# A state-space layer and a gated MLP: the last group's last product laid out by tokens, and the accumulators' copies written ahead of each group's last product

## The chip, the core and the metric

One core of a Trainium2 chip runs the whole program: TensorE (PE), which multiplies and writes its sums to PSUM; VectorE (DVE), ScalarE (ACT) and GpSimd (POOL), which compute on SBUF and PSUM; SyncE (SP), which here only issues transfers; and 16 DMA engines. The metric is the time of one execution on the device in microseconds, the median over several executions. The trace comes from one profiled execution. In it a 32-bit matmul shows as two passes, each with its weight load (PEld).

## The reference

A chunked state-space scan (4 batches, 8 heads, 768 steps, head size 32, state size 16) makes `y`; its heads, put side by side, are the 3072 tokens of 256 features that go into a two-layer network of 2048 hidden units with the activation `h * sigmoid(1.702 h)`.

```python
def reference(x, a, B, C, moe_w_in, moe_w_out):
    y = ssd(x, a, B, C)              # (4, 8, 768, 32), in chunks of 32 steps
    x = y.transpose(0, 2, 1, 3).reshape(3072, 256)
    h = x @ moe_w_in                 # (256, 2048)
    g = h * (1.0 / (1.0 + np.exp(-1.702 * h)))
    return g @ moe_w_out             # (2048, 256) -> (3072, 256)
```

All is in float32; the two weight matrices come as float64 and are made float32 on the chip.

## The kernel before

The tokens run in six groups of 512 (`TG`, `NG` = 6). For each group the scan makes `yT` (features on partitions, tokens along the row), the first layer makes the hidden blocks `gT[g, j]` (`j` from 0 to 7, 256 hidden units each), and the second layer adds eight products into accumulators in PSUM.

From group 2 on in the first layer, and from group 1 on in the second, a 2x2 block product is made with seven multiplications in place of eight. `mix_w` and `mix_g` make sums of blocks of `w_out` and of `gT` beforehand (`mw`, `mg`). `product(g, j, only)` (L809) issues the chosen ones of seven terms, each a matmul of 128x128 weights with 128 rows of 256 tokens, into seven accumulators of 128x256. For groups 1 to 4 the seven lie in one PSUM tile of four banks (`acc{g}`, from `area`, one buffer, the same that the scan's scores `cb` use). For group 5 they lie in four tiles of two. `ORDER` (L807) is 0, 1, 5, 4, 2, 3, 6. The accumulators have output features on partitions and tokens along the row.

After a group's last product, `combine(g)` (L849) makes the four output blocks. It first calls `copies(g)` (L834), in which ScalarE copies accumulators 0 and 3 from PSUM to SBUF (L840, one activation of 128x512). Then VectorE makes five sums (`plus`, L847) into `u` and `c`. `give(g)` turns the blocks of `c` back to tokens on partitions with TensorE transposes (`turn_out`, L864), scales them on ScalarE (L872) and stores them.

The order of work is written out by hand: the strings given to `run` name each step. `P` is the next product of the group before, `j.i` is term `i` of the first layer's block `j` of this group, and letters stand for other calls. `in_order` makes every engine issue its instructions in program order. In the string of L1121 the last product (`P`, term 6 of `j` = 7) stands ahead of `1.D C`: `1.D` is a VectorE sum into `gT[g, 1]`, and `C` calls `combine(g - 1)`. `block(g, 1)` takes the `gT` buffer at `1.D`; `copies` takes two more of the same six. After that come first-layer steps (`2.1 1.S 1.4 1.3 2.6 ...`, L733 and L743), and `s1`, the next scores (L546), which need the PSUM tile of the accumulators.

The last group is finished by `end` (L876). It makes the last three `j` (5, 6, 7) of all seven terms, term by term, so that the sums of one term run while TensorE makes the next. Its order of terms is 0, 3, 4, 2, 6, 1 and 5. Term 5 is made in two halves of 128 tokens (`products(5, halves[k])`), each followed by a VectorE sum of that half. Then all blocks of `c` are turned (`o[0]`: both feature blocks of the first 256 tokens; `o[2]` and `o[1]`: the two feature blocks of the last 256 tokens), scaled, and stored by three transfers: `store` from SP (L761), `put` from ScalarE's queue and `put` from SP's (L883).

Of the kernel before, what the change touches and what calls it, by code (L numbers as in the profile page):

```python
# [35 lines left out]
def kernel(  # L36
# [31 lines left out]
    nc = tc.nc  # L68
# [12 lines left out]
    NF = DF // P  # L81
    NG = T // TG
# [12 lines left out]
    ffn = ctx.enter_context(tc.tile_pool(name="ffn", bufs=2))  # L95
# [164 lines left out]
    for r in range(R):  # L260
# [22 lines left out]
                            op1=ALU.min)  # L283
# [203 lines left out]
    def bank(name):  # L487
        return ps.tile([P, 4 * P], FP32, tag="ff", name=name)
# [316 lines left out]


    ORDER = (0, 1, 5, 4, 2, 3, 6)  # L807

    def product(g, j, only=ORDER, cols=slice(0, HT)):  # L809
        if j == 0 and g not in acc:  # L810
            if g < NG - 1:
                a = area(f"acc{g}").rearrange("p r (t e) -> p (r t) e", t=2)
                acc[g] = [a[:, i] for i in range(7)], a
            else:

                areas.close()
                last = ctx.enter_context(
                    tc.tile_pool(name="last", bufs=1, space=bass.MemoryType.PSUM))
                tiles = [last.tile([P, 2, HT], FP32, name=f"acc{g}_{i}") for i in range(4)]
                acc[g] = [tiles[i // 2][:, i % 2] for i in range(7)], tiles  # L820
        B = gT[g, j].rearrange("p i (t e) -> p i t e", t=2)
        T = mixed_g[g, j]
        A, S = w_out[:, 2 * j:2 * j + 2], mixed_w[j]

        terms = ((A[:, 0, :P], B[:, 0, 0]), (A[:, 1, :P], B[:, 1, 0]), (S[:, 1], T[:, 2]),
                 (S[:, 0], T[:, 0]), (S[:, 2], T[:, 1]), (S[:, 3], B[:, 1, 1]),
                 (A[:, 1, P:], T[:, 3]))
        for i in only:
            lhsT, rhs = terms[i]
            nc.tensor.matmul(out=acc[g][0][i][:, cols], lhsT=lhsT, rhs=rhs[:, cols],  # L830
                             start=(j == 0 and i in (0, 2, 5, 6)), stop=(j == NF // 2 - 1),
                             skip_group_check=True)

    def copies(g):  # L834
        u = ffn.tile([P, 4, HT], FP32, tag="gT", name=f"u{g}", bufs=6)
        c = ffn.tile([P, 2, 2, HT], FP32, tag="gT", name=f"c{g}", bufs=6)
        done[g] = u, c

        if g < NG - 1:
            nc.scalar.activation(u[:, 0:4:3], acc[g][1][:, 0:4:3], AF.Copy)  # L840
        else:
            nc.scalar.activation(u[:, 0], acc[g][0][0], AF.Copy)
            nc.scalar.activation(u[:, 3], acc[g][0][3], AF.Copy)
        return u, c

    def plus(o, v, w):
        nc.vector.tensor_tensor(out=o, in0=v, in1=w, op=ALU.add)  # L847

    def combine(g):  # L849


        u, c = copies(g)
        a = acc[g][1]
        plus(u[:, 2], a[:, 2], u[:, 0])
        plus(u[:, 1:3], a[:, 3:5], u[:, 2:3].to_broadcast([P, 2, HT]))
        plus(c[:, 1, 1], u[:, 2], u[:, 3])
        plus(c[:, 0], a[:, 1:6:4], u[:, 0:2])
        plus(c[:, 1, 0], a[:, 6], u[:, 2])

    def turn_out(g, t, blocks, o, ks=range(2)):  # L860

        for i in blocks:
            for k in ks:
                nc.tensor.transpose(out=o[:, k, i * P:(i + 1) * P],  # L864
                                    in_=done[g][1][:, i, t, k * P:(k + 1) * P], identity=ident)

# [8 lines left out]

    def end(g, j0):  # L876

        def products(i, cols=slice(0, HT)):
            for j in range(j0, NF // 2):
                product(g, j, (i,), cols)  # L880

        def put(k0, k1, i, ob, queue):
            queue.dma_start(  # L883
                out=out[g * TG + HT + k0 * P:g * TG + HT + k1 * P, i * P:(i + 1) * P].rearrange(
                    "(k p) d -> p k d", p=P), in_=ob[:, k0:k1])

        _, p2, p6, p5, p7, p3, p4 = acc[g][0][:7]
        products(0)
        products(3)
        u, c = copies(g)  # L890
        u2, u4, u3 = u[:, 2], u[:, 1], c[:, 1, 0]
        products(4)
        products(2)
        plus(u2, p6, u[:, 0])
        plus(u4, p5, u2)
        products(6)
        plus(u3, p7, u2)
        plus(c[:, 1, 1], u3, u[:, 3])
        products(1)
        plus(c[:, 0, 0], p2, u[:, 0])  # L900
        o = [bank(f"oT{g}_{i}").rearrange("p (k e) -> p k e", k=2) for i in range(3)]
        ob = [ffn.tile([P, 2, TG], FP32, tag="gT", name=f"ob{g}_1_{i}", bufs=6)[:, :, :P]
              for i in range(2)]
        halves = [slice(k * P, (k + 1) * P) for k in range(2)]
        products(5, halves[0])
        plus(c[:, 1, 0], p4, u3)
        plus(c[:, 0, 1, halves[0]], p3[:, halves[0]], u4[:, halves[0]])
        products(5, halves[1])
        plus(c[:, 0, 1, halves[1]], p3[:, halves[1]], u4[:, halves[1]])
        turn_out(g, 0, range(2), o[0])  # L910
        half_out = out_tile(g, 0)
        nc.scalar.activation(half_out, o[0], AF.Copy, scale=1.0 / GELU_SCALE)
        store(g, 0, half_out)
        turn_out(g, 1, (1,), o[2])
        nc.scalar.activation(ob[1], o[2][:, :, P:], AF.Copy, scale=1.0 / GELU_SCALE)
        put(0, 2, 1, ob[1], nc.scalar)
        turn_out(g, 1, (0,), o[1])
        nc.vector.tensor_single_scalar(out=ob[0], in_=o[1][:, :, :P], scalar=1.0 / GELU_SCALE,
                                       op=ALU.mult)
        put(0, 2, 0, ob[0], nc.sync)  # L920


    assert PG == 2
# [166 lines left out]
    def seven(g, j):  # L1090
        return [(g, j, (i,)) for i in ORDER]

# [16 lines left out]
    for g in range(2, NG):  # L1109
        n, p = (g + 1) * PG, (g + 2) * PG  # L1110
        more, most = g + 1 < NG, g + 2 < NG
        chunks = list(range((g + 2) * CG, (g + 3) * CG)) if most else []
        rows = [b for b in range(NB) if most and (g + 2) * CG <= b * NC < (g + 3) * CG]
        if most:
            load(p)
            for c in chunks[:2]:
                spread(c)
            for b in rows:
                spread_rows(b)
        run(g, "0.1 P P 0.6 P P 0.7 P 0.5 P 0.2 P 0.D", seven(g - 1, 6))  # L1120
        run(g, "1.1 0.S P 0.4 P P 1.6 P 0.3 0.T P 1.5 P 1.7 1.2 P 1.D C", seven(g - 1, 7),  # L1121
            C=lambda: combine(g - 1))
        def along():
            for r in rows:
                clip_rows(r)
                decay_rows(r)

        def refill():
            if most:
                load(p + 1)  # L1130
                for c in chunks[2:]:
                    spread(c)

        if more:

            run(g, "2.1 1.S 1.4 1.3 2.6 2.5 2.2 2.7 1.T s1 2.D 2.S w1 give 2.4 3.1 2.3 3.5 2.T M0 3.6 "
                "s2 w2 y1 refill 3.7 3.2 3.D along 4.1 P P 3.4 P 3.S 4.6 P 3.3 4.5 3.T M1 P P y2 4.7 P 4.2 4.D M2",
                seven(g, 0), s1=lambda: score(n), w1=lambda: weigh(n), give=lambda: give(g - 1),
                s2=lambda: score(n + 1), w2=lambda: weigh(n + 1), y1=lambda: finish(n),
                refill=refill, along=along, y2=lambda: finish(n + 1), M0=lambda: mix_g(g, 0), M1=lambda: mix_g(g, 1),  # L1140
                M2=lambda: mix_g(g, 2))
            if most:
                decay(chunks[0])
        else:
# [51 lines left out]
```

## Time and profile before

| | |
|---|---|
| median of 4 runs | 374.63 us (374.59 to 374.76) |
| profiled execution: time, span of the trace | 374.6 us, 372.9 us |
| granted TensorE clock | 1.000 |
| `copies` in `combine` (L840), 4 times | 597 ns each; ScalarE idle before them 2.0 us in all, until TensorE L830 |
| VectorE's first sum (L847) after it, 4 times | idle before 1.3 us in all, until L840 |
| scores (L546) that wait for `combine`'s sums, 3 times | TensorE idle 1.1 us in all |
| products L830, `acc<-mg,mw`, 128x256 | 240 passes, mean 379 ns |
| products L830 of 128x128 in `end` | 12 passes, from 365.66 and from 366.87 us |
| the last three stores, issued | 368.95, 369.23 and 369.42 us |

How to read it: a row of the timeline has start, duration, engine, line, operation, `output<-inputs`, and in brackets how long the engine was idle before it and what ended that. Consecutive instructions of one kind are merged (`x2`), from the first start to the last end. A matmul's duration holds its way through the array, so consecutive ones overlap: 256 columns take 0.38 us each, and start 0.216 us after one another. The list of waits has the time waited in all, how often, and the longest.

### The profile page before, as it was taken

The numbers are of one execution on the slowest core, as the hardware profiler recorded it, in microseconds if no ns is written. First come the engines' busy times: TensorE is split into PE (matmuls) and PEld (weight loads), VectorE is DVE, ScalarE is ACT, GpSimd is POOL, SyncE is SP. The second block draws the span as 40 slices with busy tenths as digits, with TensorE's granted clock in tenths as the row PEclk, the third lists the DMA queues.
The fourth block names the chain that finished last, engine by engine and source line by source line (L and its number), as shares of the span: only waits on it lengthen the run. The fifth ranks groups of instructions, "written<-read, shape, count | busy, mean of one in ns | idle before, by whom it ended". The sixth has DMA issues, their size and how long they took to land.

```text
span 372.9 us, 5764 instructions
## 1 busy us (share of the span) xinstructions
PE 364.2 (98%) x2278; PEld 285.1 (76%) x2278; DVE 267.7 (72%) x439; ACT 152.0 (41%) x337; POOL 10.8 (3%) x34
## 2 busy tenths in 40 slices
PE   7999999999999999999999999999999999999995
PEld 3674468885467588778888788888878888888884
DVE  4999999998879976587886476888484355464443
ACT  5678661402331123553433554423554331554320
POOL 4200000100000010000000000000000000000000
PEclk9999999999999999999999999999999999999999
DMA  9997698806856110086300073000010000000011
GB/s 153 243 347 131 229 228 121 247 9 112 186 140 115 58 42 0 2 169 114 112 3 1 2 132 94 0 2 0 0 58 2 0 3 1 0 2 0 0 58 56
DMA packets 85795, 29.56 MB, mean 79 GB/s; under 512 B 75721, under 2 KB 79241, under 8 KB 85769
## 3 DMA queue, kind: packets, MB, share of 16 engines
q1 hardware_dynamic: 83320, 28.81, 32.8%
q10 hardware_dynamic: 2448, 0.39, 0.6%
q8 instruction: 18, 0.29, 0.3%
q14 instruction: 9, 0.07, 0.1%
HBM read 25.95 MB, written 3.24 MB: 78 GB/s over the span
## 4 chain that ended last, share of the span: by engine, by line
PE 91%; DVE 5%; ACT 2%; DMA 1%; issue 1%; ACTq 0%; DVEq 0%
PE acc L830 33%; PE X L733 13%; PE h L661 13%; PE Y L743 10%; PE o L773 8%; PE cb L546 3%; PE y L619 3%; DVE c L847 2%; PE y L610 2%; PE h L675 1%; PE ab L462 1%; PE tp L498 1%; DVE u L847 1%; PE oT L864 1%; ACT L L481 1%; PE A L574 1%
## 5 line engine op out<-in xcount | busy, mean ns | idle before, releaser
L830 PE MATMUL acc<-mg,mw 128*128 128x256 f32 x240 | 66.0, 379 | 0.0
L847 DVE TENSOR_TENSOR gT<-Y,ac 128x512 f32<-128x512 f32 x32 | 22.1, 691 | 44.3 <-PE Y L743 42.4
L738 ACT ACTIVATE ac<-X 128x256 f32<-128x256 f32 x64 | 24.6, 384 | 66.5 <-PE X L733 66.4
L830 PEld LDWEIGHTS acc<-mg,mw 128*128 128x128 f32 x240 | 45.6, 190 | 6.2
L661 PE MATMUL h<-yT,w_in 128*128 128x512 f32 x112 | 49.9, 595 | 0.0
L710 ACT ACTIVATE gT<-gT 128x512 f32<-128x512 f32 x64 | 33.3, 521 | 28.2 <-DVE gT L847 27.8
L830 PE MATMUL acc<-gT,w_out 128*128 128x256 f32 x160 | 43.8, 380 | 0.0
L347 DVE TENSOR_TENSOR_SCAN L<-a,idents 128x1024 f32<-128x1024 f32 x18 | 41.1, 2283 | 0.0
L733 PE MATMUL X<-my,mi 128*128 128x256 f32 x128 | 38.7, 384 | 0.0
L661 PEld LDWEIGHTS h<-yT,w_in 128*128 128x128 f32 x112 | 20.8, 190 | 23.4 <-issue 21.4
L830 PEld LDWEIGHTS acc<-gT,w_out 128*128 128x128 f32 x160 | 30.2, 190 | 5.5 <-issue 1.4
L847 DVE TENSOR_TENSOR gT<-Y,b 128x256 f32<-128x256 f32 x32 | 13.5, 422 | 26.7 <-PE Y L743 26.4
L664 ACT ACTIVATE gT<-h 128x512 f32<-128x512 f32 x28 | 16.6, 596 | 39.4 <-PE h L661 39.3
L773 PE MATMUL o<-w_out,gT 128*128 128x256 f32 x128 | 29.0, 382 | 0.0
L701 DVE TENSOR_TENSOR mg<-gT 128x512 f32<-128x512 f32 x40 | 27.3, 682 | 0.0
L733 PEld LDWEIGHTS X<-my,mi 128*128 128x128 f32 x128 | 23.7, 190 | 4.3 <-issue 1.2
L773 PEld LDWEIGHTS o<-w_out,gT 128*128 128x128 f32 x128 | 23.8, 190 | 4.1 <-issue 1.1
L557 DVE TENSOR_TENSOR L<-L,cb 128x2048 f32<-128x2048 f32 (+1 forms) x12 | 25.3, 2108 | 1.7 <-PE cb L546 1.6
L830 PE MATMUL acc<-gT,mw 128*128 128x256 f32 (+1 forms) x86 | 24.1, 369 | 0.4 <-DVE c L847 0.4
L830 PE MATMUL acc<-mg,w_out 128*128 128x256 f32 x80 | 23.5, 379 | 0.0
L641 ACT ACTIVATE yT<-y 128x256 f32<-128x256 f32 x22 | 7.2, 382 | 35.6 <-PE y L619 35.3
L733 PE MATMUL X<-yT,w_in 128*128 128x256 f32 x64 | 19.3, 383 | 0.0
(144 smaller groups left out, 540.3 us busy)
## 6 DMA issues: line engine op xcount, KB each, us to landing
a<-scratch SPq DMA_DIRECT2D x18, 512.0 KB, 5.8
bits<-in_moe_w_out_dram SPq DMA_DIRECT2D x4, 1024.0 KB, 7.3
x<-in_x_dram SPq DMA_DIRECT2D x24, 128.0 KB, 3.4
out_dram<-ob SPq DMA_DIRECT2D x11, 256.0 KB, 2.4
bits<-in_moe_w_in_dram SPq DMA_DIRECT2D x4, 512.0 KB, 5.5
bits<-in_moe_w_in_dram SPq DMA_DIRECT2D x2, 1024.0 KB, 9.4
b<-in_B_dram SPq DMA_DIRECT2D x24, 64.0 KB, 3.5
c<-in_C_dram SPq DMA_DIRECT2D x22, 64.0 KB, 2.5
```

Of the source, the lines that this page charges most:

```text
L347: nc.vector.tensor_tensor_scan(out=Ls[p][:, k].rearrange("p r q i -> p (r q i)"), data0=ra[n], data1=idents.rearrange("p h i -> p (h i)"), ...
L557: nc.vector.tensor_tensor(out=Lv[:, k], in0=Lv[:, k], in1=cb.rearrange("p r k e -> p k r e")[:, k], op=ALU.mult)
L661: nc.tensor.matmul(out=h, lhsT=w_in[:, k, f * P:(f + 1) * P], rhs=yT[g][:, k], start=(k == 0), stop=(k == NK - 1))
L664: nc.scalar.activation(gT[g, j][:, i], h, AF.Silu, scale=GELU_SCALE)
L701: nc.vector.tensor_tensor(out=t[:, 0:2], in0=B[:, :, 1], in1=B[:, 0], op=ALU.subtract)
L710: nc.scalar.activation(o, i, AF.Silu, scale=GELU_SCALE)
L733: nc.tensor.matmul(out=s["X"], lhsT=lhsT, rhs=rhs, start=i == "1", stop=i == "4", skip_group_check=True)
L738: nc.scalar.activation(copy, s["X"], AF.Copy)
L743: nc.tensor.matmul(out=o, lhsT=lhsT, rhs=rhs, start=s.pop("new", False), stop=i != "5", skip_group_check=True)
L773: nc.tensor.matmul(out=o[k // 2][:, k % 2], lhsT=gT[g, f // 2][:, f % 2, k * P:(k + 1) * P], rhs=w_out[:, f], start=(f == 0 and k % 2 == 0 ...
L830: nc.tensor.matmul(out=acc[g][0][i][:, cols], lhsT=lhsT, rhs=rhs[:, cols], start=(j == 0 and i in (0, 2, 5, 6)), stop=(j == NF // 2 - 1), ...
L847: nc.vector.tensor_tensor(out=o, in0=v, in1=w, op=ALU.add)
```

## The change

In `end`, and in every `product` of group 5, term 5 is now made with the operands exchanged: the tokens' 128x128 block is the stationary operand and the weights move, so that the accumulator has tokens on partitions and features along the row, in two matmuls of 128 columns for the two halves of the tokens. Its addend `u4` is turned with two transposes, copied and scaled by ScalarE into a buffer (`ob[2]`), and one VectorE operation (`scalar_tensor_tensor`) scales the accumulator and adds the addend, straight into the tile that is stored. The halves' sums and the turn of that block are gone.

The order in `end` is changed: after term 5's first `j` come the turns and copies of the addend and of the other three blocks, with their two stores; then term 5's last two `j`; then the VectorE step and the last store. The sum with `p4` comes ahead of term 1. The output tiles use the buffers `b` and `ac` in place of `gT`.

In the groups before, `copies(g - 1)` is called by a step of its own, `U`, which stands ahead of the last product; `combine` uses what it has made.

```diff
     ORDER = (0, 1, 5, 4, 2, 3, 6)
-    def product(g, j, only=ORDER, cols=slice(0, HT)):
+    LAST = 5
+    def product(g, j, only=ORDER):
...
         for i in only:
             lhsT, rhs = terms[i]
-            nc.tensor.matmul(out=acc[g][0][i][:, cols], lhsT=lhsT, rhs=rhs[:, cols],
-                             start=(j == 0 and i in (0, 2, 5, 6)), stop=(j == NF // 2 - 1),
+            start, stop = j == 0 and i in (0, 2, 5, 6), j == NF // 2 - 1
+            if g == NG - 1 and i == LAST:
+                for k in range(2):
+                    cols = slice(k * P, (k + 1) * P)
+                    nc.tensor.matmul(out=acc[g][0][i][:, cols], lhsT=rhs[:, cols], rhs=lhsT,
+                                     start=start and k == 0, stop=stop, skip_group_check=True)
+                continue
+            nc.tensor.matmul(out=acc[g][0][i], lhsT=lhsT, rhs=rhs, start=start, stop=stop,
                              skip_group_check=True)
...
     def combine(g):
-        u, c = copies(g)
+        u, c = done[g]
...
     def end(g, j0):
-        def products(i, cols=slice(0, HT)):
+        def products(i):
             for j in range(j0, NF // 2):
-                product(g, j, (i,), cols)
+                product(g, j, (i,))
...
         plus(c[:, 1, 1], u3, u[:, 3])
+        plus(c[:, 1, 0], p4, u3)
         products(1)
         plus(c[:, 0, 0], p2, u[:, 0])
+        product(g, j0, (LAST,))
         o = [bank(f"oT{g}_{i}").rearrange("p (k e) -> p k e", k=2) for i in range(3)]
-        ob = [ffn.tile([P, 2, TG], FP32, tag="gT", name=f"ob{g}_1_{i}", bufs=6)[:, :, :P]
-              for i in range(2)]
-        halves = [slice(k * P, (k + 1) * P) for k in range(2)]
-        products(5, halves[0])
-        plus(c[:, 1, 0], p4, u3)
-        plus(c[:, 0, 1, halves[0]], p3[:, halves[0]], u4[:, halves[0]])
-        products(5, halves[1])
-        plus(c[:, 0, 1, halves[1]], p3[:, halves[1]], u4[:, halves[1]])
+        ob = [ffn.tile([P, HT], FP32, tag="b", name=f"ob{g}_1_{i}").rearrange(
+            "p (k e) -> p k e", k=2) for i in range(2)]
+        ob.append(ffn.tile([P, 2, HT], FP32, tag="ac", name=f"uT{g}")[:, :, :P])
+        for k in range(2):
+            nc.tensor.transpose(out=o[1][:, k, :P], in_=u4[:, k * P:(k + 1) * P], identity=ident)
+        nc.scalar.activation(ob[2], o[1][:, :, :P], AF.Copy, scale=1.0 / GELU_SCALE)
+        turn_out(g, 1, (1,), o[2])
+        nc.scalar.activation(ob[1], o[2][:, :, P:], AF.Copy, scale=1.0 / GELU_SCALE)
+        put(1, ob[1], nc.scalar)
         turn_out(g, 0, range(2), o[0])
         half_out = out_tile(g, 0)
         nc.scalar.activation(half_out, o[0], AF.Copy, scale=1.0 / GELU_SCALE)
         store(g, 0, half_out)
-        turn_out(g, 1, (1,), o[2])
-        nc.scalar.activation(ob[1], o[2][:, :, P:], AF.Copy, scale=1.0 / GELU_SCALE)
-        put(0, 2, 1, ob[1], nc.scalar)
-        turn_out(g, 1, (0,), o[1])
-        nc.vector.tensor_single_scalar(out=ob[0], in_=o[1][:, :, :P], scalar=1.0 / GELU_SCALE,
-                                       op=ALU.mult)
-        put(0, 2, 0, ob[0], nc.sync)
+        for j in range(j0 + 1, NF // 2):
+            product(g, j, (LAST,))
+        nc.vector.scalar_tensor_tensor(
+            out=ob[0], in0=p3.rearrange("p (k e) -> p k e", k=2), scalar=1.0 / GELU_SCALE,
+            in1=ob[2], op0=ALU.mult, op1=ALU.add)
+        put(0, ob[0], nc.sync)
...
-        run(g, "1.1 0.S P 0.4 P P 1.6 P 0.3 0.T P 1.5 P 1.7 1.2 P 1.D C", seven(g - 1, 7),
-            C=lambda: combine(g - 1))
+        run(g, "1.1 0.S P 0.4 P P 1.6 P 0.3 0.T P 1.5 P 1.7 1.2 U P 1.D C", seven(g - 1, 7),
+            U=lambda: copies(g - 1), C=lambda: combine(g - 1))
```

More of the change, by code (lines that the diff above doesn't have):

```diff
@@ L858, in combine, with turn_out @@
         plus(c[:, 1, 0], a[:, 6], u[:, 2])
-    def turn_out(g, t, blocks, o, ks=range(2)):
+    def turn_out(g, t, blocks, o):
         for i in blocks:
-            for k in ks:
+            for k in range(2):
                 nc.tensor.transpose(out=o[:, k, i * P:(i + 1) * P],
@@ L876, in end, with put @@
     def end(g, j0):
-        def products(i, cols=slice(0, HT)):
+        def products(i):
             for j in range(j0, NF // 2):
-                product(g, j, (i,), cols)
[L882 to L885, printed above, removed]
+                product(g, j, (i,))
+        def put(i, ob, queue):
+            queue.dma_start(out=out[g * TG + HT:(g + 1) * TG, i * P:(i + 1) * P].rearrange(
+                "(k p) d -> p k d", p=P), in_=ob)
         _, p2, p6, p5, p7, p3, p4 = acc[g][0][:7]
@@ L898, in end @@
         plus(c[:, 1, 1], u3, u[:, 3])
+        plus(c[:, 1, 0], p4, u3)
         products(1)
         plus(c[:, 0, 0], p2, u[:, 0])
+        product(g, j0, (LAST,))
         o = [bank(f"oT{g}_{i}").rearrange("p (k e) -> p k e", k=2) for i in range(3)]
-        ob = [ffn.tile([P, 2, TG], FP32, tag="gT", name=f"ob{g}_1_{i}", bufs=6)[:, :, :P]
-              for i in range(2)]
-        halves = [slice(k * P, (k + 1) * P) for k in range(2)]
-        products(5, halves[0])
-        plus(c[:, 1, 0], p4, u3)
-        plus(c[:, 0, 1, halves[0]], p3[:, halves[0]], u4[:, halves[0]])
-        products(5, halves[1])
-        plus(c[:, 0, 1, halves[1]], p3[:, halves[1]], u4[:, halves[1]])
+        ob = [ffn.tile([P, HT], FP32, tag="b", name=f"ob{g}_1_{i}").rearrange(
+            "p (k e) -> p k e", k=2) for i in range(2)]
+        ob.append(ffn.tile([P, 2, HT], FP32, tag="ac", name=f"uT{g}")[:, :, :P])
+        for k in range(2):
+            nc.tensor.transpose(out=o[1][:, k, :P], in_=u4[:, k * P:(k + 1) * P], identity=ident)
[3 more added lines that the diff above has]
+        put(1, ob[1], nc.scalar)
         turn_out(g, 0, range(2), o[0])
```

## The prediction

> **What bounds the kernel now.** I read the page's busy times and chain first, then the waits in total, then the order of time around the places that the diff touches.
>
> ```profile
> PE 364.2 (98%) x2278; PEld 285.1 (76%) x2278; DVE 267.7 (72%) x439; ACT 152.0 (41%) x337; POOL 10.8 (3%) x34
> ...
> PE 91%; DVE 5%; ACT 2%; DMA 1%; issue 1%; ACTq 0%; DVEq 0%
> ```
>
> TensorE is the bound: 98% busy and 91% of the chain. So an edit counts if it adds or removes time in TensorE's stream, or in the last microseconds behind its last matmul. The waits between 150 and 330 us show the few places where the stream breaks:
>
> ```profile
> ACT u L840 <- PE acc L830: 2.0, 4, 0.5
> DVE u L847 <- ACT u L840: 1.3, 4, 0.4
> ...
> PE cb L546 <- DVE c L847: 1.1, 3, 0.4
> ...
> PEld Y L743 <- DVE gT L847: 0.5, 1, 0.5
> ```
>
> Four times, once per group, the accumulators' copy (L840) waits for the group's last product (L830), VectorE's sums wait for the copy, and TensorE waits for the sums. Here is the first of the four in order of time:
>
> ```profile
> 151.99 0.38 ACT L738 ACTIVATE ac<-X 128x256 f32<-128x256 f32 x1 [0.85 <-PE X L733]
> ...
> 152.22 0.59 PE L830 MATMUL acc<-mg,w_out 128*128 128x256 f32 x2
> ...
> 152.49 0.69 DVE L847 TENSOR_TENSOR gT<-Y,ac 128x512 f32<-128x512 f32 x1 [1.80 <-PE Y L743]
> 152.65 0.59 PE L733 MATMUL X<-yT,w_in 128*128 128x256 f32 x2
> ...
> 152.91 0.60 ACT L840 ACTIVATE u<-acc 128x512 f32<-128x512 f32 x1 [0.54 <-PE acc L830]
> ...
> 153.54 1.15 DVE L847 TENSOR_TENSOR u<-acc,u 128x256 f32<-128x256 f32 x2 [0.36 <-ACT u L840]
> ...
> 155.07 1.01 DVE L847 TENSOR_TENSOR c<-acc,u 128x512 f32<-128x512 f32 x2
> ...
> 155.24 0.59 PE L733 MATMUL X<-my,mi 128*128 128x256 f32 x2
> ...
> 156.23 1.15 PE L546 MATMUL cb<-CT,BT 32*128 32x256 f32 x16 [0.40 <-DVE c L847]
> ```
>
> A product of 256 columns is two passes and takes 0.43 (152.22 to 152.65). The copy reads accumulators 0 and 3 only, yet it starts 0.10 after the end (152.81) of the product into accumulator 6: the program guards the tile of accumulators as one. TensorE should go on at 155.24 + 0.43 = 155.67 and goes on at 156.23: 0.56 lost. The group's second score, which meets no wait, still starts 0.09 late (160.58), so 0.47 can be won here. The same windows at 213.27 and 270.31 give 0.50 and 0.49, so 0.40 each. In the last group the break is elsewhere:
>
> ```profile
> 326.26 0.70 PE L743 MATMUL Y<-my,mi 128*128 128x256 f32 x2
> ```
>
> It was due at 325.53 + 0.43 = 325.96, so it is 0.30 late; its pair took 0.70, not 0.59, because after a break the second weight load is no longer hidden: 0.11 more, 0.41 in all. The four breaks are worth 0.47 + 0.40 + 0.40 + 0.41 = 1.68. The end of the kernel:
>
> ```profile
> 365.66 0.83 PE L830 MATMUL acc<-gT,mw 128*128 128x128 f32 x6
> ...
> 366.87 0.94 PE L830 MATMUL acc<-gT,mw 128*128 128x128 f32 x6 [0.38 <-DVE c L847]
> ...
> 367.64 1.04 PE L864 MATMUL oT<-ident,c 128*128 128x128 f32 x8
> ...
> 368.33 0.60 ACT L912 ACTIVATE ob<-oT 128x512 f32<-128x512 f32 x1 [7.27 <-PE oT L864]
> 368.72 0.42 DVE L918 TENSOR_SCALAR ob<-oT 128x256 f32<-128x256 f32 x1 [0.58 <-PE oT L864]
> 368.82 0.38 ACT L915 ACTIVATE ob<-oT 128x256 f32<-128x256 f32 x1
> 368.95 0.37 SPq L761 DMA_DIRECT2D out_dram<-ob  x1
> 369.23 0.39 ACTq L883 DMA_DIRECT2D out_dram<-ob  x1
> 369.42 0.42 SPq L883 DMA_DIRECT2D out_dram<-ob  x1
> ```
>
> The last store is issued at 369.42 although its data were ready at 368.72 + 0.42 = 369.14: SP was still issuing the store before it (368.95 + 0.37 = 369.32, plus 0.09 to the next). It lands 2.64 later (the DMA view's 2.6), and the span ends 0.82 after that.
>
> **The copies written ahead (four places).** The instruction lists of the two built programs show what the diff doesn't say: the copy loses its wait for the last product, and the last product gains a wait for ScalarE's copy, since it writes the tile that the copy reads. VectorE's first sum now waits for that product. No ScalarE instruction changes places. So TensorE's stream gets a wait where it had none. Its price, from the first place: the copy can start when ScalarE has taken the activation of 151.99; a 128x256 one lets the next start 0.26 later (153.41 to 153.67), so at 152.25, and with its 0.60 it ends at 152.85. TensorE takes up an instruction freed by ScalarE 0.05 later (153.79 to the weight load at 153.84): 152.90, not 152.22. With 0.11 for the exposed weight load the stream is 0.79 late. The other three have the same spacing (209.09 and 209.32 for L738 and the product; 321.84 and 322.07): 4 x 0.79 = 3.16.
>
> Queued behind the held product are the next blocks' first-layer products (L733, L743) and then the scores; ScalarE's L738 and VectorE's gT sums wait for those, and all move with TensorE. What is late next? The sums start 0.05 after the product's new end, 152.90 + 0.70 = 153.60, so at 153.65 against 153.54 before, and the last sum ends 0.11 later (156.09 to 156.20). TensorE gets to the scores at 155.67 + 0.79 + 0.09 = 156.55, so the old break is covered: its 1.68 comes back. Net 3.16 - 1.68 = +1.48. Bounds: the copy could start or be seen 0.08 earlier or later at each place, +1.15 to +1.80; if TensorE did not feel the wait at all, -1.68.
>
> The Trainium skill speaks against the need for this wait (PSUM — Partial Sum Buffer, section "PSUM bank collisions raise a hardware error"): two engines must be kept apart within a bank, not within a tile. Its specifications give a bank 512 f32 values, so accumulators 0, 3 and 6 lie in three banks, and by the rule the product could run beside the copy: the sum would be the -1.68 case. The program has the wait all the same, so I go by the rows. Also moved are the buffers: u and c take their gT buffers before the next gT block does. Every earlier reader of those buffers is a product or sum of the group before, done microseconds earlier, and no new wait for them is in the lists: 0.
>
> **The product by tokens.** Five products (j 0 to 4) that were two passes of 256 columns (2 x 0.216) become four of 128. Six passes of 128 end in 0.83, one alone takes 0.27, so a pass is 0.56 / 5 = 0.11 (0.1115 unrounded): 0.446 against 0.432, +0.014 each, +0.07. Bounds 0 and +0.2 (if each change of width exposed half a weight load).
>
> **The end.** Counted from 365.66, where the last product begins in both. TensorE: four passes for j 5, to 366.10; two turns of the addend at 0.109, to 366.32; two of c's last block, 366.54; four of c's first half, 366.98; eight passes, 367.87, done 0.16 later at 368.03. Gone are the wait of 0.55 at 366.87 (the second half waited for VectorE's read of the first) and the two turns of the last block; the sum with p4 moves ahead, where VectorE is idle before 365.86. All the turns' sources are done by 366.28 (the p2 sum, 365.86 + 0.42). VectorE's last step is then ready at 368.07 and, at 0.43 (L918's row; its new operation on 128x128 took 0.35, on 128x512 0.71), done at 368.50.
>
> But ScalarE and SP now carry the end: the addend's copy starts at 366.21 + 0.27 + 0.10 = 366.58, the next at 366.85, ending at 367.23; then ScalarE issues its store, 0.39, before it makes the first half: 367.65, plus 0.10 for two semaphore steps, plus 0.60 gives 368.35. SP issues that store at 368.38, is free at 368.75, and issues the last one 0.09 later, at 368.84. VectorE's 368.50 is hidden under that. 368.84 - 369.42 = -0.58. If ScalarE's issue ran beside its activation, VectorE would decide and the issue be near 368.55; if the stores crowd each other less, the last may land in the 2.4 that the page has for the kernel's other stores: together -1.1. On the other side, another 0.2 between ScalarE's steps: -0.4.
>
> The Trainium skill (DMA: Bandwidth & Descriptors, section "Anatomy of one DMA") has about 2.0 us fixed plus bytes over 436 GB/s, fitted on another issue path; for 128 KB that estimates 2.3, under the 2.64 here. With 2.3 the end would be 0.34 earlier still. The sum keeps 2.64.
>
> **Sum.** +1.48 + 0.07 - 0.58 = +0.97. The profiled execution took 374.6 with a span of 372.9 (1.7 lie around it) and the median is 374.63, so both give 375.6.
>
> **Rivals.**
> 1. The hold is felt, but the end gains its -1.1 and the hold only its low bound: 1.15 + 0.07 - 1.1 = +0.1, or in parts up to +0.6: 374.7 to 375.2. For it: the last store was held by SP alone. Against: ScalarE's store issue now stands ahead of the big activation.
> 2. The other side, faster: TensorE runs on, because the copy is out of the way before the product comes. It decides as soon as the copy ends before 152.17; then the four breaks go with nothing in exchange: -1.68 + 0.07 - 0.58 = -2.2, 372.4. For it: every break hangs on the copy's late start. Against: the copy cannot start before 151.99, as ScalarE waits there for X, and it lasts 0.60.
> 3. The end gains nothing: ScalarE's issue delays the first half's store and the last store queues behind it, at 369.4 as before: +1.55, 376.2. For it: three stores still pass two issuing engines. Against: TensorE is done 0.65 earlier.
>
> **How the numbers follow.** A measurement of this kernel tells about 0.2%, 0.75 us, from no change. The forecast has 0.72, its own range 375.1 to 376.0, with some 0.08 of it under 375.38; rival 1 has 0.13, rival 2 0.08, rival 3 0.07. Slower: 0.64 + 0.07 = 0.71; within: 0.08 + 0.13 = 0.21; faster: 0.08. The range 375.0 to 376.1 leaves out rival 2, most of rival 1 and the edge of rival 3.
>
> **What would show it.** In the changed profile: the last product of groups 1 to 4 idles some 0.5 to 0.7, with ScalarE's u as releaser; the copy starts 0.26 after L738; no break remains ahead of the scores; the last store is issued after ScalarE's first-half activation, not after VectorE's step. No idle time ahead of that product would make the forecast wrong, as would a last store that waits for VectorE.

## The result and the profile after

| | before | after |
|---|---|---|
| median of 52 and of 34 runs | 374.72 us | 375.28 us |
| ratio, 95% interval | | 1.0016 [1.0012, 1.0021] |
| profiled execution: time, span | 374.6, 372.9 us | 375.2, 373.5 us |

The change costs some 0.6 us: slower, by less than the 0.2% (0.75 us) that the prediction had set as the bound of "no change". The forecast of 375.6 had the sign and the mechanism, but its amount was too large: +0.97, where the medians differ by 0.56 and the spans of the two traces by 0.62. The time lies in the stated range of 375.0 to 376.1, in its part under 375.38, which the forecast had given 0.08. The chance of 0.71 stood on "slower by over 0.2%", which did not come.

The page of the kernel after, busy times and chain:

```profile
PE 365.1 (98%) x2288; PEld 284.9 (76%) x2288; DVE 267.6 (72%) x437; ACT 151.5 (41%) x338; POOL 10.8 (3%) x34
...
PE 94%; DVE 2%; ACT 2%; DMA 1%; issue 0%; ACTq 0%; DVEq 0%
```

TensorE is still 98% busy, but its share of the chain has grown from 91 to 94% and VectorE's has fallen from 5 to 2%. The waits of VectorE are off the path, and yet the time is longer: what replaced them has to be looked for in front of TensorE. In the list of waits from 150 to 330 us (engine, line, what ended the wait, total, times, longest):

```profile
PEld acc L839 <- ACT u L848: 3.7, 4, 0.9
...
DVE gT L855 <- ACT ac L738: 2.3, 4, 0.6
PE acc L839 <- ACT u L848: 2.1, 4, 0.5
DVE u L855 <- PE acc L839: 1.9, 4, 0.5
```

Line numbers moved: the product is L839 (L830 before), the copy L848 (L840), the sums L855 (L847). Before, the copy waited for the product (2.0 in all) and the sums for the copy. Now the product waits for the copy, four times, and the sums wait for the product. The wait of the scores (L546) for the sums is gone from the list. The first place in order of time:

```profile
152.00 0.38 ACT L738 ACTIVATE ac<-X 128x256 f32<-128x256 f32 x1 [0.85 <-PE X L733]
152.28 0.59 ACT L848 ACTIVATE u<-acc 128x512 f32<-128x512 f32 x1
...
152.92 0.30 PEld L839 LDWEIGHTS acc<-mg,w_out 128*128 128x128 f32 x2 [0.93 <-ACT u L848]
152.92 0.70 PE L839 MATMUL acc<-mg,w_out 128*128 128x256 f32 x2 [0.53 <-ACT u L848]
...
153.66 1.15 DVE L855 TENSOR_TENSOR u<-acc,u 128x256 f32<-128x256 f32 x2 [0.47 <-PE acc L839]
...
156.57 1.15 PE L546 MATMUL cb<-CT,BT 32*128 32x256 f32 x16
```

The copy starts 0.28 after the activation ahead of it, ends at 152.87, and 0.05 later the product starts, 0.69 after its place. Its pair takes 0.70 instead of 0.59: the weight load that nothing hid. The scores at 156.57 carry no bracket: TensorE comes to them without a wait. The end of the kernel:

```profile
367.34 0.61 PE L836 MATMUL acc<-mw,gT 128*128 128x128 f32 x4
...
368.26 0.38 ACT L917 ACTIVATE uT<-oT 128x256 f32<-128x256 f32 x1 [5.52 <-PE oT L916]
368.54 0.38 ACT L919 ACTIVATE ob<-oT 128x256 f32<-128x256 f32 x1
...
368.95 0.39 ACTq L891 DMA_DIRECT2D out_dram<-ob  x1
369.44 0.60 ACT L923 ACTIVATE ob<-oT 128x512 f32<-128x512 f32 x1 [0.53 <-ACT ob L919]
369.83 0.42 DVE L927 SCALAR_TENSOR_TENSOR ob<-acc,uT 128x256 f32<-128x256 f32 x1 [1.86 <-PE acc L836]
370.07 0.37 SPq L761 DMA_DIRECT2D out_dram<-ob  x1
370.53 0.42 SPq L891 DMA_DIRECT2D out_dram<-ob  x1
```

Term 5 (L836) starts at 367.34 where it started at 365.66 before, and the last store is issued at 370.53 instead of 369.42. The DMA view puts its landing at 2.6 us behind its issue before, and at 2.1 after:

```profile
out_dram<-ob SPq DMA_DIRECT2D x1, 128.0 KB, 2.1
```

In what follows a landing is the moment at which SP's wait for the last store ends, as in the prediction: 0.82 before the end of the span in every trace, and 0.02 behind the landing of the DMA view. By it the two are 2.64 and 2.15.

So the account between the two traces has three entries. TensorE comes to term 5 of `end` late by 367.34 - 365.66 = +1.68. From there to the last store's issue takes 3.195 (367.338 to 370.533) instead of 3.759 (365.659 to 369.418), -0.56. From that issue to the landing takes 2.15 instead of 2.64, -0.49. The sum is +0.63; the spans, 372.88 and 373.50, differ by 0.62.

### The profile page after: what moved, and what is told of

It reads as the page before. It is cut to its first block, busy times and chain, and to the rows that moved or that the text cites. A ratio compares the mean times of both kernels' runs of the same rounds, so it can differ in the third digit from the quotient of the medians.

```text
span 373.5 us, 5786 instructions
## 1 busy us (share of the span) xinstructions
PE 365.1 (98%) x2288; PEld 284.9 (76%) x2288; DVE 267.6 (72%) x437; ACT 151.5 (41%) x338; POOL 10.8 (3%) x34
## 4 chain that ended last, share of the span: by engine, by line
PE 94%; DVE 2%; ACT 2%; DMA 1%; issue 0%; ACTq 0%; DVEq 0%
PE acc L839 32%; PE X L733 15%; PE h L661 13%; PE Y L743 11%; PE o L773 8%; PE cb L546 3%; PE y L619 3%; PE y L610 2%; PE h L675 1%; PE ab L462 1%; PE tp L498 1%; PE oT L872 1%; PE acc L836 1%; ACT L L481 1%; PE A L574 1%; DMA az<-in_a_dram 1%
## 5 line engine op out<-in xcount | busy, mean ns | idle before, releaser
L839 PE MATMUL acc<-mg,mw 128*128 128x256 f32 x240 | 66.0, 379 | 0.0
L855 DVE TENSOR_TENSOR gT<-Y,ac 128x512 f32<-128x512 f32 x32 | 22.1, 692 | 46.3 <-PE Y L743 42.4
L839 PEld LDWEIGHTS acc<-mg,mw 128*128 128x128 f32 x240 | 45.5, 190 | 6.1
L839 PE MATMUL acc<-gT,w_out 128*128 128x256 f32 x160 | 43.8, 380 | 0.0
L839 PEld LDWEIGHTS acc<-gT,w_out 128*128 128x128 f32 x160 | 30.2, 190 | 5.5 <-issue 1.4
L855 DVE TENSOR_TENSOR gT<-Y,b 128x256 f32<-128x256 f32 x32 | 13.5, 421 | 26.7 <-PE Y L743 26.4
L839 PE MATMUL acc<-mg,w_out 128*128 128x256 f32 x80 | 23.9, 384 | 2.1 <-ACT u L848 2.1
L839 PE MATMUL acc<-gT,mw 128*128 128x256 f32 x64 | 19.3, 384 | 0.0
```

What stands on the lines that cost most here:

```text
L839: nc.tensor.matmul(out=acc[g][0][i], lhsT=lhsT, rhs=rhs, start=start, stop=stop, skip_group_check=True)
```

## The experiments

Each kernel ran in five rounds beside the kernel before on the same chip; a ratio compares the runs of the two kernels in those rounds, has its 95% interval in brackets, and need not equal the quotient of the two medians. `e1` to `e4`, `e5` to `e8`, and `e9` with `e10` ran on three different chips, so runs of different sets are compared by their traces. All of them compute the whole result.

### The tail alone, and the copies alone

`e1_tail_only` is the kernel after with the copies back in `combine`:

```diff
-        u, c = done[g]
+        u, c = copies(g)
...
-        run(g, "1.1 0.S P 0.4 P P 1.6 P 0.3 0.T P 1.5 P 1.7 1.2 U P 1.D C", seven(g - 1, 7),
-            U=lambda: copies(g - 1), C=lambda: combine(g - 1))
+        run(g, "1.1 0.S P 0.4 P P 1.6 P 0.3 0.T P 1.5 P 1.7 1.2 P 1.D C", seven(g - 1, 7),
+            C=lambda: combine(g - 1))
```

> The changed kernel with the accumulators' copies back behind each group's last product; the product by tokens and the new end stay. My theory: the hold of the last product is what costs, and the end gains. The four holds (0.80 each) go and the four breaks (1.68 in all) come back, so this is 1.5 us under the changed kernel and about 1.0 us (0.9 to 1.2) under the kernel before: 373.6 to 373.8. Rival: the copies written ahead were near neutral and the end itself is what lost; then this stays within 0.3 us of the changed kernel, above the kernel before.

Measured: 373.77 against 374.82, ratio 0.9975 [0.9966, 0.9985], span 371.9. The waits of the kernel before are all back, here as this kernel's list has them:

```profile
ACT u L848 <- PE acc L839: 2.0, 4, 0.5
DVE u L855 <- ACT u L848: 1.3, 4, 0.4
...
PE cb L546 <- DVE c L855: 1.1, 3, 0.4
```

`e2_copies_only` is the kernel before with the step `U` alone:

```diff
-        u, c = copies(g)
+        u, c = done[g]
...
-        run(g, "1.1 0.S P 0.4 P P 1.6 P 0.3 0.T P 1.5 P 1.7 1.2 P 1.D C", seven(g - 1, 7),
-            C=lambda: combine(g - 1))
+        run(g, "1.1 0.S P 0.4 P P 1.6 P 0.3 0.T P 1.5 P 1.7 1.2 U P 1.D C", seven(g - 1, 7),
+            U=lambda: copies(g - 1), C=lambda: combine(g - 1))
```

> The kernel before with only the copies written ahead of each group's last product. My theory: four holds of 0.80 in, four breaks of 1.68 out, so 1.5 us (1.3 to 1.7) above the kernel before: about 376.2. Rival: the copies are neutral or gain, within 0.3 us of the kernel before or under it.

Measured: 376.20 against 374.82, ratio 1.0042 [1.0029, 1.0054], span 374.5. With the end unchanged, one mark can be followed through: the last matmuls of `end`, which started at 366.87, start at 368.47 (366.872 to 368.466, +1.59):

```profile
368.47 0.94 PE L830 MATMUL acc<-gT,mw 128*128 128x128 f32 x6 [0.38 <-DVE c L847]
```

The two parts have opposite signs. The new end and the product by tokens alone gain 0.99 us in the trace (372.88 to 371.89); the copies written ahead alone lose 1.59. The small result of the whole is the difference of two larger effects.

### The copy written sooner

If the hold is only the copy's late start, then two steps earlier should bring the faster side of the prediction's rivals. `e3_copy_sooner` is the kernel after with `U` moved ahead of `1.7 1.2`:

```diff
-        run(g, "1.1 0.S P 0.4 P P 1.6 P 0.3 0.T P 1.5 P 1.7 1.2 U P 1.D C", seven(g - 1, 7),
+        run(g, "1.1 0.S P 0.4 P P 1.6 P 0.3 0.T P 1.5 P U 1.7 1.2 P 1.D C", seven(g - 1, 7),
```

> The changed kernel with the copies two first-layer steps sooner, right after the product into accumulator 3 (term 3). The last product still waits for the copy, but the copy now ends at about 152.15 in the first place, where the product is due at 152.22. My theory: of each hold 0.0 to 0.2 is left and the sums start 0.45 sooner than before, so that the four breaks stay closed: 2.4 to 3.2 us under the changed kernel, 372.0 to 372.9. Rival: the wait itself costs (a stop of the queue with its exposed weight load, or a copy that now delays the activation behind it and what needs that), and less than 1 us of the hold goes: above 374.2.

Measured: 372.45 against 374.82, ratio 0.9944 [0.9931, 0.9958], span 370.7.

```profile
151.61 0.60 ACT L848 ACTIVATE u<-acc 128x512 f32<-128x512 f32 x1 [0.48 <-PE acc L839]
...
152.10 0.38 ACT L738 ACTIVATE ac<-X 128x256 f32<-128x256 f32 x1
152.25 0.30 PEld L839 LDWEIGHTS acc<-mg,w_out 128*128 128x128 f32 x2 [0.28 <-ACT u L848]
152.25 0.70 PE L839 MATMUL acc<-mg,w_out 128*128 128x256 f32 x2
```

The copy ends at 152.20, and 0.05 later the product starts, 0.05 after its place (1.295 behind the product before it, as in the kernel before: 152.21); the exposed load costs 0.10 more. At the other three places the copy ends sooner, 0.07 ahead of the product's place. There the product starts on time, yet its weight load, which in the kernel before starts 0.21 ahead of it, still waited for the copy, and the second pass is 0.09 late:

```profile
208.98 0.30 PEld L839 LDWEIGHTS acc<-mg,w_out 128*128 128x128 f32 x2 [0.23 <-ACT u L848]
209.00 0.69 PE L839 MATMUL acc<-mg,w_out 128*128 128x256 f32 x2
```

So 0.15 + 3 x 0.09 = 0.42 us of the holds are left. `e5_three_steps` moves one more step, so that two products stand between the copy and the last one:

```diff
-        run(g, "1.1 0.S P 0.4 P P 1.6 P 0.3 0.T P 1.5 P 1.7 1.2 U P 1.D C", seven(g - 1, 7),
+        run(g, "1.1 0.S P 0.4 P P 1.6 P 0.3 0.T P P U 1.5 1.7 1.2 P 1.D C", seven(g - 1, 7),
```

> The kernel with the copies sooner (e3), and one step more between the copy and the last product: two products follow each other, then the copy, then three first-layer steps. In e3 the last product still starts 0.04 late and pays 0.11 for an exposed weight load, four times. My theory: that goes, 0.4 to 0.6 us under e3: 371.9 to 372.1. Rival: what is left in e3 is no hold of this product (another wait takes its place, the copy now being in the way of the activation behind it), and the time stays within 0.2 of e3's 372.45.

Measured: 372.15 against 374.68, ratio 0.9930 [0.9917, 0.9942], span 370.3.

```profile
151.19 0.60 ACT L848 ACTIVATE u<-acc 128x512 f32<-128x512 f32 x1
...
152.22 0.59 PE L839 MATMUL acc<-mg,w_out 128*128 128x256 f32 x2
```

The product starts at 152.22 with no wait and takes 0.59: hold and exposed load are both gone. The trace gained 0.39 over `e3_copy_sooner`, near the 0.42 that was left there. The expectation of 0.4 to 0.6 had counted 0.15 at all four places, and three of them cost 0.09. The median, 0.30 lower, is just outside it; those two were taken on different chips, and their intervals overlap, so it is the trace that shows the gain. Against `e1_tail_only`, where the copy stands behind the last product, the span is 1.56 shorter: the breaks are gone, and hardly anything was paid for them.

### Matmuls of 128 columns

The term for the five products in two halves was small and rested on a spacing read from merged rows. `e4_halves` multiplies it: the kernel before, with term 5 of groups 1 to 4 in two matmuls of 128 columns, 32 products instead of five:

```diff
-            nc.tensor.matmul(out=acc[g][0][i][:, cols], lhsT=lhsT, rhs=rhs[:, cols],
-                             start=(j == 0 and i in (0, 2, 5, 6)), stop=(j == NF // 2 - 1),
-                             skip_group_check=True)
+            for sl in ((slice(0, P), slice(P, HT)) if g < NG - 1 and i == 5 else (cols,)):
+                nc.tensor.matmul(out=acc[g][0][i][:, sl], lhsT=lhsT, rhs=rhs[:, sl],
+                                 start=(j == 0 and i in (0, 2, 5, 6) and sl.start == 0),
+                                 stop=(j == NF // 2 - 1), skip_group_check=True)
```

> The kernel before with term 5 of groups 1 to 4 in two matmuls of 128 columns, 32 products in place of the five of the change, operands not exchanged. My theory: 0.014 each, +0.45 us in all (0.2 to 0.7), 375.2. Rival: each change of width exposes part of a weight load, 0.1 a product, +3 us, and then the five of the change cost 0.5.

Measured: 375.19 against 374.82, ratio 1.0016 [1.0007, 1.0024]. TensorE's mark in `end` moves from 366.872 to 367.454, 0.58 / 32 = 0.018 for one product. Five cost 0.09. `e1_tail_only`, which has the five products themselves, gives nearly the same: its term 5 in `end` starts at 365.728 instead of 365.659, +0.07. The theory of an exposed load at each change of width, which would have cost some 3 us here, falls.

### The stores at the end

Why did the last store land 0.49 sooner after its issue? It may be that stores crowd each other, or that only the queue matters which issues them. `e6_sp_store` is `e3_copy_sooner` with the first store of the end issued by SP, so that ScalarE's big activation need not stand behind an issue:

```diff
-        put(1, ob[1], nc.scalar)
+        put(1, ob[1], nc.sync)
```

> The kernel with the copies sooner (e3), with the first of the last three stores issued by SP in place of ScalarE. My theory: ScalarE's issue (0.39 and its steps) stands ahead of the first half's activation and holds its store and so the last one; without it the last store is issued as soon as VectorE is done, 0.25 sooner: 372.2. Rival: the last store's issue hangs on TensorE and VectorE and nothing moves (372.45), or the three stores in one queue land later and it is slower (372.6).

Measured: 372.19 against 374.68, ratio 0.9931 [0.9917, 0.9944], span 370.2. The median is the expected one, but the trace (of an execution of 371.91, the fastest of five) shows something else. The last store is issued 0.25 sooner, as expected, but the 256 KB store (L761), the big one, 0.54 sooner, at 366.75 instead of 367.29, since the big activation no longer waits behind ScalarE's issue. Here it is in `e3_copy_sooner`, then in this kernel:

```profile
366.66 0.60 ACT L923 ACTIVATE ob<-oT 128x512 f32<-128x512 f32 x1 [0.53 <-ACT ob L919]
```

```profile
366.13 0.60 ACT L923 ACTIVATE ob<-oT 128x512 f32<-128x512 f32 x1
```

The span is 0.53 shorter. The end followed the big store, not the last one.

`e7_late_store` was to bring the stores together: `e3_copy_sooner` with the store kept on ScalarE and written behind the big activation.

```diff
-        put(1, ob[1], nc.scalar)
         turn_out(g, 0, range(2), o[0])
         half_out = out_tile(g, 0)
         nc.scalar.activation(half_out, o[0], AF.Copy, scale=1.0 / GELU_SCALE)
         store(g, 0, half_out)
+        put(1, ob[1], nc.scalar)
```

> The kernel with the copies sooner (e3), with the first of the last three stores issued by ScalarE behind the first half's activation in place of ahead of it, so that the three stores leave within 0.85 us as in the kernel before (0.47), not within 1.6. The open question is why the last store landed 2.15 after its issue in the changed kernel and 2.64 in the kernel before. If the stores crowd each other: 384 KB at the 340 GB/s that the trace shows need 1.13 us, so the last one waits some 0.3 and lands 2.4 to 2.5 after its issue; the issue is 0.25 sooner, the time 372.4 to 372.6. If the landing doesn't depend on the others: 2.15 and 372.2.

Measured: 372.12 against 374.68, ratio 0.9935 [0.9922, 0.9947]. The expectation was missed, because the experiment did not make what it was meant to make:

```profile
366.26 0.60 ACT L922 ACTIVATE ob<-oT 128x512 f32<-128x512 f32 x1
366.35 0.39 ACTq L891 DMA_DIRECT2D out_dram<-ob  x1
366.89 0.37 SPq L761 DMA_DIRECT2D out_dram<-ob  x1
```

ScalarE issued its store at 366.35, in the middle of the activation of 366.26 that stands ahead of it. The store still left 0.54 ahead of the big one, so nothing was crowded, and about crowding the run says nothing.

`e8_both` joins the two that gained, `e5_three_steps` and the store on SP:

```diff
-        put(1, ob[1], nc.scalar)
+        put(1, ob[1], nc.sync)
...
-        run(g, "1.1 0.S P 0.4 P P 1.6 P 0.3 0.T P 1.5 P 1.7 1.2 U P 1.D C", seven(g - 1, 7),
+        run(g, "1.1 0.S P 0.4 P P 1.6 P 0.3 0.T P P U 1.5 1.7 1.2 P 1.D C", seven(g - 1, 7),
```

> Three steps between copy and last product (e5) and the first store issued by SP (e6), with the rest of the change. The two savings are at different places and add: 0.4 to 0.6 and 0.25 under e3's 372.45, so 371.6 to 371.8, 3.0 us under the kernel before. Rival: one of the two does not hold, 372.0 or above.

Measured: 371.68 against 374.68, ratio 0.9919 [0.9905, 0.9932], as expected. Its traced execution is the slowest of its four, 371.98.

`e9_crowded` is `e8_both` with the block's activation and its store behind the big one, on ScalarE, so that the store can't leave before the activation has made its data:

```diff
-        nc.scalar.activation(ob[1], o[2][:, :, P:], AF.Copy, scale=1.0 / GELU_SCALE)
-        put(1, ob[1], nc.sync)
         turn_out(g, 0, range(2), o[0])
         half_out = out_tile(g, 0)
         nc.scalar.activation(half_out, o[0], AF.Copy, scale=1.0 / GELU_SCALE)
         store(g, 0, half_out)
+        nc.scalar.activation(ob[1], o[2][:, :, P:], AF.Copy, scale=1.0 / GELU_SCALE)
+        put(1, ob[1], nc.scalar)
```

> e8 with the first half's activation and store ahead, and the other block's activation and 128 KB store behind them (from ScalarE), so that the big store and two small ones leave within 0.8 us as in the kernel before. So far the last store lands 2.62 after the big store's issue in e1, e3, e6, e7, e8 and the changed kernel, however late its own issue (0.46 to 0.75 after the big one), and 3.11 after it in the kernel before, where 128 KB more lie between them. My theory: the stores' bytes behind the big store's issue set the end; with the 128 KB between again the last one lands 3.0 to 3.1 after the big store's issue, +0.4 us on e8: 372.0 to 372.2. Rival: another cause (the queue, the last store's own issue); then 2.6 and 371.7.

Measured: 372.20 against 374.80, ratio 0.9943 [0.9927, 0.9959]. The two ends side by side, first `e8_both`:

```profile
366.22 0.37 SPq L891 DMA_DIRECT2D out_dram<-ob  x1
366.80 0.37 SPq L761 DMA_DIRECT2D out_dram<-ob  x1
...
367.56 0.37 SPq L891 DMA_DIRECT2D out_dram<-ob  x1
```

and `e9_crowded`:

```profile
366.46 0.37 SPq L761 DMA_DIRECT2D out_dram<-ob  x1
366.74 0.39 ACTq L891 DMA_DIRECT2D out_dram<-ob  x1
...
367.22 0.37 SPq L891 DMA_DIRECT2D out_dram<-ob  x1
```

In `e9_crowded` the big store leaves 0.34 sooner and the last store 0.34 sooner, and yet the last lands at 369.57 instead of 369.44. What differs is that both small stores now follow the big one. The medians of these two come from different chips and their intervals overlap, so the traces carry this comparison. Over all the traces, with the landing of the last store counted from the big store's issue and from its own:

| kernel | behind the big store | from the big store's issue | from its own issue |
|---|---|---|---|
| before, `e2_copies_only`, `e4_halves` | 2 x 128 KB | 3.09 to 3.11 | 2.62 to 2.64 |
| `e9_crowded` | 2 x 128 KB | 3.10 | 2.35 |
| after, `e1_tail_only`, `e3_copy_sooner`, `e5_three_steps`, `e10_own_tile` | 128 KB | 2.61 to 2.62 | 2.15 to 2.16 |
| `e6_sp_store`, `e7_late_store`, `e8_both` | 128 KB | 2.62 to 2.64 | 1.87 to 1.88 |

The third column takes two values, one for each amount that follows the big store; the fourth moves with the last store's own issue. So the end of this kernel is set by the big store's issue and by what is sent behind it, 0.47 to 0.49 us for 128 KB, and not by when the last store is issued, as long as that is within the 0.75 of the big one that these runs reach. The queue that issues the first small store makes no difference: ScalarE's in `e7_late_store` and SP's in `e6_sp_store` give the same two times. 128 KB in 0.47 to 0.49 us is some 270 to 280 GB/s, an estimate; in the DMA view of the kernel before from 365 to 373.6 us, the four full slices behind the peak show 277 to 291 GB/s. That is near enough to speak for the bytes as the cause, but the runs do not separate the bytes from the number of stores.

### Accumulator 6 in a tile of its own

If the guard of one tile makes the hold, then the copy where the change put it should do no harm once the last product writes another tile. `e10_own_tile` is the kernel after with the fourth bank as a tile of its own; the scan's scores, which use the same space, are then written into two tiles and read by VectorE in two operations:

```diff
-        return psa.tile([P, R, 4 * P], FP32, tag="cb", name=name)
+        return (psa.tile([P, R - 1, 4 * P], FP32, tag="cb", name=name),
+                psa.tile([P, 1, 4 * P], FP32, tag="cbl", name=f"{name}l"))
...
-                a = area(f"acc{g}").rearrange("p r (t e) -> p (r t) e", t=2)
-                acc[g] = [a[:, i] for i in range(7)], a
+                a, b = (x.rearrange("p r (t e) -> p (r t) e", t=2) for x in area(f"acc{g}"))
+                acc[g] = [a[:, i] for i in range(6)] + [b[:, 0]], a
...
-        plus(c[:, 1, 0], a[:, 6], u[:, 2])
+        plus(c[:, 1, 0], acc[g][0][6], u[:, 2])
```

> The changed kernel with accumulator 6 (one bank of the four) in a tile of its own; the copies stand where the change put them. The last product then needs no wait for the copy, and the copy none for the product. The scores use the same two tiles, so that VectorE's weighting is two operations (3/4 and 1/4) in place of one. My theory: the hold is made by the tile that the two share, not by the chip; the four holds (0.80 each) go, the breaks stay closed: 3.0 to 3.3 us under the changed kernel, 372.0 to 372.4, plus up to 0.5 for the added VectorE operations. Rival: writing one bank while ScalarE reads others slows the product or the copy, or the breaks come back: above 373.

Measured: 373.76 against 374.80, ratio 0.9972 [0.9963, 0.9981], span 372.2. The place in question does what the theory says:

```profile
153.89 0.39 ACT L745 ACTIVATE ac<-X 128x256 f32<-128x256 f32 x1 [0.85 <-PE X L740]
...
154.12 0.59 PE L846 MATMUL acc1l<-mg,w_out 128*128 128x256 f32 x2
154.17 0.59 ACT L855 ACTIVATE u<-acc 128x512 f32<-128x512 f32 x1
```

The product starts 0.23 after the activation ahead of the copy, as in the kernel before, and the copy runs beside it. From this product to the end of the span it is 372.22 - 154.12 = 218.10, against 373.50 - 152.23 (the product's place) = 221.27 in the kernel after: -3.17, where four holds of 0.80 come to 3.19. The total missed its forecast by over 0.8 us, since this kernel is already 1.9 late at its first product here. That is lost between 20 and 60 us, long before any copy. The first row is that stretch in the kernel after, the second in `e10_own_tile` (the stretch, its length, then the busy time of TensorE with its instructions, and of the weight loads, VectorE, ScalarE and GpSimd; the granted clock, the DMA share and GB/s come last):

```profile
20.00:60.00 40.00, 39.60 (x190) 23.90 (x189) 38.77 (x55) 27.46 (x41) 1.10 (x3) 1.00 0.87 227
```

```profile
20.00:60.00 40.00, 37.93 (x181) 22.32 (x181) 37.05 (x55) 27.62 (x41) 1.16 (x3) 1.00 0.83 223
```

TensorE does 1.67 us less work there. One longer wait of its first layer for VectorE (2.4 instead of 0.7) stands in this stretch; how the second tile brings it about was not followed further.

## Why the prediction was right in kind and wrong in size

**The hold: right.** The product was forecast 0.79 late at each place. It is 0.69 of waiting and 0.10 of exposed load, 0.797 unrounded, at each of the four places; the copy starts at 152.28 (forecast 152.25), the product at 152.92 (152.90), the sums at 153.66 (153.65). The cause was put down to the guard of one tile; `e10_own_tile` shows it, as the hold disappears where the copy and the product use different tiles, and `e3_copy_sooner` and `e5_three_steps` show the other half, that the copy stood too late for the product. The Trainium skill (PSUM — Partial Sum Buffer, section "PSUM bank collisions raise a hardware error") asks that engines be kept apart by bank. The run with its own tile agrees: the copy (154.17) and the product (154.12), which use different banks, work at the same time.

**The breaks won back: right, slightly too large.** No wait for `combine`'s sums is left ahead of the scores. `e2_copies_only` gives +1.59 for holds and breaks together. Four holds measure 3.19 (4 x 0.797), so 1.60 came back and not 1.68. The net was forecast +1.48; this is 0.11 of error against the kernel.

**The products in two halves: right.** +0.07 forecast, 0.07 by `e1_tail_only` and 0.09 by `e4_halves`. With the copies written ahead, 1.59 + 0.09 = 1.68, which is the delay of term 5 in the trace of after.

**The end up to the last issue: right.** -0.58 forecast, -0.56 measured. Moved by the 1.68, the prediction's moments are 368.26 for the addend's copy, 369.43 for the big activation, 370.06 for its store and 370.52 for the last; the trace has 368.26, 369.44, 370.07 and 370.53. ScalarE's issue ahead of the activation carries this end, and VectorE's step, done at 370.25, is hidden under SP.

**The landing: the step that failed.** The sum kept the 2.64 of the last store of the kernel before as if it belonged to any last store of 128 KB. It belonged to three stores issued within 0.47, the big one first. The change sends one of them 1.12 ahead of the big one (368.95 and 370.07), and the time from the last store's issue to its landing falls to 2.15. This is the mis-sized term: 0 in the sum, -0.49 in the trace. The prediction named it ("if the stores crowd each other less") but only as the low bound of the end, and with a floor of 2.4. `e9_crowded` shows that it is what follows the big store: with both small stores behind it again, the 3.10 from the big store's issue returns. The Trainium skill's estimate for one transfer (DMA: Bandwidth & Descriptors, section "Anatomy of one DMA"), about 2.0 us and the bytes over 436 GB/s, fitted on another issue path than these stores take, gives 2.3 for 128 KB. It was nearer to the 2.15 than 2.64 was, but no run here has one figure for such a store: it took from 1.87 to 2.64, by what was on its way ahead of it.

**The sum.** +1.48 + 0.07 - 0.58 + 0 = +0.97 became 1.59 + 0.09 - 0.56 - 0.49 = +0.63. The errors in the copies' term (+0.11) and in the landing (-0.49) have opposite signs and partly cancel, which is luck; the larger one carried the result under the 0.75 bound.

**The rivals.** Rival 1 (a small hold and a large gain at the end) ends near the right time, at most 375.2, with only one of its two halves true: the end gained 1.05 of its 1.1, but the copies cost 1.59, more than their forecast, not their low bound of 1.15. And the end gained it by another split: 0.56 at the issue and 0.49 at the landing, where the prediction had 0.87 (369.42 - 368.55) and 0.24 (2.64 - 2.4). Rival 2 (faster, 372.4, with a copy out of the way before 152.17) did not happen here, and its condition was the right one: `e5_three_steps` ends the copy at 151.79 and takes 372.15. Its span, 2.55 under the kernel before, is close to the 2.58 of the breaks (1.60) and the end (1.05), less 0.07 for the products in halves. Rival 3 (the end gains nothing) is excluded by `e1_tail_only`.

**A better version.** `e8_both` keeps the new end, writes the copy three steps sooner and issues all three stores from SP: 371.68, ratio 0.9919 [0.9905, 0.9932], 3.0 us under the kernel before and 3.6 under the kernel after. That it is better than `e5_three_steps` and `e6_sp_store` alone is not settled, since their intervals overlap with its own.

## What to carry to other kernels

Where two instructions share a tile, moving one ahead of the other in program order turned their wait around here rather than removing it: ask when the moved one can start, and whether it ends before the one that now waits for it is due. Here a copy that started 1.09 us sooner (152.28 and 151.19) turned a loss of 1.6 us into a gain of the same size. Or give the two a tile each, as `e10_own_tile` did at these places, and look at what else that tile is used for. At the end of this kernel the landing counted from the largest of the last stores and what was sent behind it, and a small store was better sent ahead of the large one; look for the same where a kernel ends in several stores.

## What the runs showed that was not expected

A store's issue on ScalarE costs differently by where it stands. Behind an activation it ran beside it (`e7_late_store`: issued at 366.35 for 0.39, during the activation from 366.26 to 366.86), where ScalarE had nothing more to do. Ahead of one it held it: in the kernel after it is issued from 368.95 to 369.34, and the next activation starts at 369.44. With that store on SP the activation starts 0.53 sooner, as `e6_sp_store` and `e3_copy_sooner` show above.

After a wait, TensorE loses some 0.10 us more than the wait itself, at the second weight load of the pair: 0.10 at the holds, and still 0.09 at three places of `e3_copy_sooner` where only the weight load waited and the product itself started on time.
